# Attention steps on one rotating pool of five PSUM banks, values last in the first two batches, loads staged behind the weights

## The chip, the core and the metric

The kernel runs on one core of a Trainium2 chip. The metric is device time in microseconds (us) of one launch. A profiled execution gives a page and a trace besides. In them PE is TensorE's matmuls, PEld its weight loads, DVE VectorE, ACT ScalarE, POOL GpSimd and SP SyncE, which here only issues DMAs.

## What is computed

Windowed attention for 8 batches of 8 heads, 576 positions, 64 numbers a head, and behind it a two-layer network with a swish on all 4608 tokens (2048 inner columns):

```python
scores = scale * np.matmul(q, k.transpose(0, 1, 3, 2))
rel = pos[:, None] - pos[None, :]
mask_plain = (rel >= 0) & (rel < window)                                    # heads 0 to 3, window 32
mask_dil = (rel >= 0) & (rel < window * dilation) & (rel % dilation == 0)   # heads 4 to 7, dilation 4
scores = np.where(masks[None, :, :, :], scores, -1000000000.0)
attn = softmax(scores)            # written out in the reference
x = (attn @ v), heads side by side, one row a token
h = x @ w_in
out = (h * (1.0 / (1.0 + np.exp(-beta * h)))) @ w_out
```

q, k, v, w_in, w_out and the result are float32; the kernel multiplies in bfloat16.

## The kernel before

**Attention** of one batch is a list of 42 steps, `STEPS` (L16), each named by a letter, a pair of heads (0 and 1 plain, 2 and 3 dilated) and a block. `K` and `Q` (`step_k` L220, `step_q` L229) transpose keys or queries by eight small matmuls into a PSUM bank and copy them out, K on DVE, Q on ACT or DVE by the pair's parity. `S` (L235) multiplies two blocks of scores, takes the exponential on ACT (L255) into `pt`, and multiplies by a mask of zeros and ones on POOL (L256). `V` (L261) multiplies `pt` with values that carry a column of ones, so that the row sums come along, and divides on DVE (L274, L278). `X` (L282) transposes the result, and ACT copies it into `xT`, the input of the network. An `X` needs the `V` steps of its rows; a `V` needs the masks of its scores and the values.

**The network** works in 9 tiles of 512 tokens. A tile has 16 slots `slot_h` (L307: four matmuls, tanh on ACT, L315, and one DVE instruction, L318, that makes `g`) and 16 slots `slot_o` (L333: four matmuls each, four slots to one output block, then a copy on ACT, L346, and a store by SP). `at_once` (L419) says how many of a tile's four output blocks are done within the tile itself; the rest is carried to the next tile. So tile 0 has 16 + 12 slots, tile 1 has 16 + 4 + 8, tile 2 has 16 + 8 + 4, tiles 3 to 6 have 32.

**Order.** Batch 0's attention runs by itself. Then tile t runs slot by slot, and the steps of batch t + 1 are put between the slots in proportion (`room`, `WORK`, L420 to L446), done two slots before the tile's end. Each engine executes its instructions in program order, and the order is that of the program text (`manual_schedule`). Waits are set where an instruction needs data or a buffer that another engine still uses.

**PSUM** has eight banks: `psum_h` 2, `psum_o` 1, `psum_sc` 2 for scores, `psum_pv` 1 for values, `psum_tp` 2 for K, Q and X (L68 to L72).

**Loads.** The plain half of q and k is loaded as float32 by SP into `k_st`, `q_st` and cast by DVE (batch 0) or POOL (L165). The dilated half is loaded and cast in one by POOL's DMAs into `kb`, `qb` (L162). Values are loaded by SP into `vp_st` and `vd_st` (L177, L181, L182) and cast by POOL (`cast_v`, L184); a plain block needs 32 rows of the block before it, which `fill_v` copies from SBUF to SBUF (L192). The weights are loaded and cast by POOL's DMAs, w_in in four pieces (L142) and w_out in four (L147); a piece serves four slots `slot_h`, or one of the four parts of an output block. `extras` (L359) and `first` (L402) hang the loads and casts of later batches on steps: the dilated k of the next batch at `S00`, for instance, and its values two batches ahead.

## Time and profile before

| | |
|---|---|
| time, median of 3 runs | 402.52 us (402.02 to 403.48) |
| the profiled execution's own time | 402.45 us |
| its span | 400.5 us |
| PE busy | 329.2 us, 82% |
| weight loads busy | 173.7 us, 43% |
| DVE busy | 209.0 us, 52% |
| ACT busy | 203.9 us, 51% |
| POOL busy | 168.8 us, 42% |
| read from HBM, written | 39.33 MB, 9.44 MB |

Shares are of the whole span. The span is what the profiler saw from the first instruction to the last; the time of a run has a little around it. A row of a group of instructions reads: line, engine, operation, output<-input, shape, count, then busy time and mean ns of one, then the engine's idle time before them and what ended it. A row of the timeline has its start and length first, and in brackets the idle time before it with the engine that ended it. Matmul ends are modelled, so a busy PE isn't PE at its peak. An average over the span hides that the kernel has stages with different limits.

### The profile page before, as it was taken

The numbers are of one execution on the slowest core, as the hardware profiler recorded it, in microseconds if no ns is written. First come the engines' busy times: TensorE is split into PE (matmuls) and PEld (weight loads), VectorE is DVE, ScalarE is ACT, GpSimd is POOL, SyncE is SP. The second block draws the span as 40 slices with busy tenths as digits, with TensorE's granted clock in tenths as the row PEclk, the third lists the DMA queues.
The fourth block names the chain that finished last, engine by engine and source line by source line (L and its number), as shares of the span: only waits on it lengthen the run. The fifth ranks groups of instructions, "written<-read, shape, count | busy, mean of one in ns | idle before, by whom it ended". The sixth has DMA issues, their size and how long they took to land.

```text
span 400.5 us, 6792 instructions
## 1 busy us (share of the span) xinstructions
PE 329.2 (82%) x2561; PEld 173.7 (43%) x2561; DVE 209.0 (52%) x432; ACT 203.9 (51%) x390; POOL 168.8 (42%) x225
## 2 busy tenths in 40 slices
PE   0525586598898998799989998999899989999995
PEld 0413343254554554355445444544454444444442
DVE  6723377153775586466646664675467544424400
ACT  1413166154765577367636664666466645535521
POOL 8089631885278168407840874077024300000000
PEclk9999999699999999999999999999999999999999
DMA  7979998816731637327333744350000111010022
GB/s 161 208 168 199 210 209 211 201 45 152 182 57 44 164 40 198 103 79 153 112 92 88 139 125 101 82 86 28 28 26 28 26 47 34 26 54 26 26 62 71
DMA packets 47872, 40.96 MB, mean 102 GB/s; under 512 B 22480, under 2 KB 38368, under 8 KB 47840
## 3 DMA queue, kind: packets, MB, share of 16 engines
q1 hardware_dynamic: 37216, 31.62, 30.6%
q0 software_dynamic: 10624, 8.92, 14.8%
q8 instruction: 20, 0.33, 0.4%
q14 instruction: 12, 0.10, 0.1%
HBM read 39.33 MB, written 9.44 MB: 122 GB/s over the span
## 4 chain that ended last, share of the span: by engine, by line
PE 56%; DVE 12%; DMA 10%; ACT 9%; SPq 7%; issue 4%; POOL 1%; ACTq 0%; POOLq 0%
PE o_ps L341 24%; PE h_ps L310 21%; DMA vp_st<-in_v_dram 8%; SPq L177 6%; DVE g L318 5%; ACT tnh L315 4%; PE pv L271 3%; DVE xs L278 3%; PE sc L253 2%; DVE qz L217 2%; PE tp L208 2%; PE h_ps L341 2%; PE tp L287 2%; ACT qz L214 1%; ACT pt L255 1%
## 5 line engine op out<-in xcount | busy, mean ns | idle before, releaser
L318 DVE SCALAR_TENSOR_TENSOR g<-tnh,h_ps 128x512 bf16<-128x512 bf16 x144 | 98.5, 686 | 116.9 <-ACT tnh L315 116.0
L310 PE MATMUL h_ps<-xT,w_in_bf 128*128 128x512 bf16 x576 | 149.1, 385 | 4.6 <-DVE g L318 4.2
L341 PE MATMUL o_ps<-w_out_bf,g 128*128 128x512 bf16 x544 | 137.0, 379 | 2.7 <-ACT osb L346 2.7
L315 ACT ACTIVATE tnh<-h_ps,beta_half 128x512 bf16<-128x512 f32 x144 | 98.5, 688 | 75.7 <-PE h_ps L310 75.1
L310 PEld LDWEIGHTS <-w_in_bf 128*128 128x128 bf16 x576 | 52.4, 99 | 51.5 <-issue 8.7
L341 PEld LDWEIGHTS <-g 128*128 128x128 bf16 x576 | 51.8, 98 | 51.0 <-issue 3.7
L255 ACT ACTIVATE pt<-sc 128x288 bf16<-128x288 f32 (+1 forms) x112 | 49.5, 444 | 33.9 <-PE sc L253 30.9
L256 POOL TENSOR_TENSOR pt<-pt,mask_d 128x288 bf16<-128x288 bf16 x64 | 46.5, 729 | 35.9 <-ACT pt L255 34.9
L271 PEld LDWEIGHTS <-pt 128*128 128x128 bf16 x448 | 23.9, 100 | 63.6 <-DVE xs L278 29.0
L278 DVE TENSOR_TENSOR xs<-pv,rcp 72x256 bf16<-72x256 f32 (+1 forms) x96 | 44.6, 465 | 3.3
L274 DVE RECIPROCAL rcp<-pv 72x4 f32<-72x4 f32 (+1 forms) x96 | 17.2, 179 | 44.7 <-PE pv L271 44.7
L253 PE MATMUL sc<-qz,kT 128*128 128x144 bf16 (+1 forms) x224 | 36.7, 248 | 0.0
L271 PE MATMUL pv<-vd,pt 128*128 128x65 bf16 x256 | 20.0, 200 | 17.7 <-DVE xs L278 14.8
L346 ACT ACTIVATE osb<-o_ps 128x512 f32<-128x512 f32 x34 | 20.4, 600 | 26.2 <-PE o_ps L341 26.2
L271 PE MATMUL pv<-vp,pt 128*128 128x65 bf16 x192 | 12.8, 202 | 21.0 <-POOL pt L256 15.2
L256 POOL TENSOR_TENSOR pt<-pt,mask_PP 128x384 bf16<-128x384 bf16 x32 | 28.6, 913 | 3.2 <-ACT pt L255 3.0
L162 POOL DMA_DIRECT2D kb<-in_k_dram x8 | 6.3, 790 | 54.9 <-PE tp L208 54.1
L297 ACT COPY xT<-tp 128x288 bf16<-128x288 bf16 x32 | 12.7, 397 | 32.7 <-PE tp L287 32.7
L253 PEld LDWEIGHTS <-kT 128*128 128x128 bf16 x224 | 20.4, 103 | 17.1 <-issue 0.5
L287 PE MATMUL tp<-ident_b,xs 72*128 72x72 bf16 (+1 forms) x224 | 21.3, 208 | 5.2 <-DVE xs L278 5.2
L208 PE MATMUL tp<-ident_b,kb 72*128 72x72 bf16 x256 | 14.8, 205 | 10.6 <-DVE kb L169 8.9
L188 POOL CAST vd<-vd_st 128x2048 bf16<-128x2048 f32 x8 | 15.2, 1898 | 19.2 <-PE pv L271 10.9
(52 smaller groups left out, 233.4 us busy)
## 6 DMA issues: line engine op xcount, KB each, us to landing
k_st<-in_k_dram SPq DMA_DIRECT2D x8, 576.0 KB
q_st<-in_q_dram SPq DMA_DIRECT2D x8, 576.0 KB
vp_st<-in_v_dram SPq DMA_DIRECT2D x32, 144.0 KB, 10.1
vd_st<-in_v_dram SPq DMA_DIRECT2D x8, 512.0 KB, 7.0
vd_st<-in_v_dram SPq DMA_DIRECT2D x8, 384.0 KB, 4.7
kb<-in_k_dram POOLq DMA_DIRECT2D x8, 288.0 KB, 5.1
qb<-in_q_dram POOLq DMA_DIRECT2D x8, 288.0 KB, 5.7
w_in_bf<-in_moe_w_in_dram POOLq DMA_DIRECT2D x4, 512.0 KB, 12.1
```

The source lines that it names most:

```text
L177: e(h4).dma_start(out=vp_st[WIN:P, :, h4, :], in_=v[b, h4].rearrange("(i p) d -> p i d", p=QT))
L208: nc.tensor.transpose(tv[:, n], in_, ident_b[0:RT, 0:RT])
L253: nc.tensor.matmul(sc[:, a, 0:2 * n], lhsT=lhsT, rhs=rhs, start=True, stop=True)
L255: nc.scalar.activation(out=w, in_=sc[:, :, 0:2 * n], func=ACT.Exp, scale=SCALE)
L256: nc.gpsimd.tensor_tensor(out=w, in0=w, in1=mask, op=ALU.mult)
L271: nc.tensor.matmul(pv[:, a, h2, :], lhsT=pt[x][:, c:c + P], rhs=rhs, start=True, stop=True)
L278: nc.vector.tensor_tensor(out=xs_t[b, x, jx][:, a0:a0 + m], in0=pv[0:n, :, :, 0:D], in1=rcp[0:n, 0:m].unsqueeze(3).to_broadcast([n, m, 2, ...
L287: nc.tensor.transpose(xp[:, a * n:(a + 1) * n], xs[:, a].rearrange("p h d -> p (h d)"), ident_b[0:n, 0:n])
L310: nc.tensor.matmul(hps[:], lhsT=w_in_bf[:, kt, fb * P:(fb + 1) * P], rhs=xT[:, kt, t * NTOK:(t + 1) * NTOK], start=(kt == 0), stop=(kt == ...
L315: nc.scalar.activation(out=tnh[:], in_=hps[:], func=ACT.Tanh, scale=beta_half[:, fb:fb + 1])
L318: nc.vector.scalar_tensor_tensor(out=g[:], in0=tnh[:], scalar=1.0, in1=hps[:], op0=ALU.add, op1=ALU.mult)
L341: nc.tensor.matmul(ops[:], lhsT=g_t[t, fb][:, tb * P:(tb + 1) * P], rhs=w_out_bf[:, fb, :], start=(fb == 0), stop=(fb == NFB - 1))
```

## The change

- One pool `psum_at` of five banks, taken in turn by every attention step (`bank()`), takes the place of `psum_sc`, `psum_pv` and `psum_tp`. In tile 0 two of three `slot_h` take their bank there too.
- Batches 0 and 1 follow a second list, `STEPS_FIRST`: keys, queries and scores first, values last. Later batches keep `STEPS`.
- In batches 0 and 1 the masks are applied on DVE. In batch 0 all Q copies and the casts of q go to ACT, the casts of v stay on POOL; in batch 1 ACT casts v, at `S23` and `S33`.
- `fill_v` goes: plain values are loaded with all 128 rows of a block, overlap included.
- The weights are all issued by POOL in one go, w_in's first piece behind the first cast of v, the rest behind the second. Batch 1's loads come behind two gates: small DMAs on SP that wait for `g` of slot 1 and of slot 5 of tile 0. Batch 1's q and k are cast at slot 10; batch 2's plain q and k are loaded at slot 18.
- Batch 0's and 1's q and k are loaded in two pieces of 64 and 8 rows.
- Tile 0 does all its output slots itself (32 slots; tile 1 has 24), and batch 1's steps begin at slot 14.
- For later batches, `cast_v` moves into the batch's own `K0` and `K1`, the values of the next batch are loaded at `K2`, both dilated loads at `Q3`.

```diff
+STEPS_FIRST = (
+    "K0 Q0 K1 S00 Q1 S01 K2 S02 Q2 S10 S11 K3 S12 Q3 S20 S21 S22 S23 S30 V00 S31 V01 S32 X00 "
+    "V10 S33 X01 V11 V20 X10 V21 X11 V22 X20 V23 V30 X21 V31 V32 X30 V33 X31"
 ).split()
...
+    FROM = 14
+    GATES = (1, 5)
...
     psum_h = psum("psum_h", 2)
     psum_o = psum("psum_o", 1)
-    psum_sc = psum("psum_sc", 2)
-    psum_pv = psum("psum_pv", 1)
-    psum_tp = psum("psum_tp", 2)
+    psum_at = psum("psum_at", 5)
+
+    def bank(dt=FP32):
+        b = psum_at.tile([P, 512], FP32, name="at")
+        return b[:] if dt == FP32 else b[:].bitcast(BF16)
...
-        nc.vector.memset(vp_st[0:WIN], 0.0)
+        nc.vector.memset(vp_st[0:WIN, 0, 0], 0.0)
...
         if h == 0:
-            stage[b, kind] = stage_pool.tile([RT, 4, R * D], FP32, name=f"{kind}_st")
-            nc.sync.dma_start(out=stage[b, kind][:], in_=src)
-        else:
-            qkb[b, h, kind] = qkb_pool.tile([RT, 4, R * D], BF16, name=f"{kind}b1")
-            nc.gpsimd.dma_start(out=qkb[b, h, kind][:], in_=src)
+            dst = stage[b, kind] = stage_pool.tile([RT, 4, R * D], FP32, name=f"{kind}_st")
+            eng = nc.sync
+        else:
+            dst = qkb[b, h, kind] = qkb_pool.tile([RT, 4, R * D], BF16, name=f"{kind}b1")
+            eng = nc.gpsimd
+
+        for lo, hi in ((0, 64), (64, RT)) if b < 2 else ((0, RT),):
+            eng.dma_start(out=dst[lo:hi], in_=src[lo:hi])
...
             for h4 in range(4):
-                e(h4).dma_start(
-                    out=vp_st[WIN:P, :, h4, :], in_=v[b, h4].rearrange("(i p) d -> p i d", p=QT))
+                if b or h4:
+                    src = bass.AP(tensor=v.tensor, offset=v[b, h4].offset - WIN * D,
+                                  ap=[[D, P], [QT * D, NI], [1, D]])
+                    e(h4).dma_start(out=vp_st[:, :, h4, :], in_=src)
+                else:
+                    src = v[b, h4].rearrange("(i p) d -> p i d", p=QT)
+                    e(h4).dma_start(out=vp_st[WIN:P, :, h4, :], in_=src)
+                    e(h4).dma_start(out=vp_st[0:WIN, 1:NI, h4, :], in_=src[QT - WIN:QT, 0:NI - 1])
...
-    def fill_v(b):
-        va = vp[b % 2]
-        nc.sync.dma_start(out=va[0:WIN, 1:NI], in_=va[96:128, 0:NI - 1])
+
+    def gate(t, fb):
+        nc.sync.dma_start(out=gate_t[:], in_=g_t[t, fb][0:1, 0:16])
...
-        copy = nc.vector.tensor_copy if x % 2 else nc.scalar.copy
+        copy = nc.vector.tensor_copy if b and x % 2 else nc.scalar.copy
...
-        sc = psum_sc.tile([P, 2, 256], FP32, name="sc")
+        sc = bank().rearrange("p (a n) -> p a n", a=2)
...
-        nc.gpsimd.tensor_tensor(out=w, in0=w, in1=mask, op=ALU.mult)
+        eng = nc.gpsimd if b > 1 else nc.vector
+        eng.tensor_tensor(out=w, in0=w, in1=mask, op=ALU.mult)
...
-        hps = psum_h.tile([P, NTOK], FP32, name="h_ps")
+        hps = bank() if t == 0 and fb % 3 else psum_h.tile([P, NTOK], FP32, name="h_ps")[:]
...
     def extras(b):
         e = {}
-        at = lambda name, fn: e.setdefault(STEPS.index(name), []).append(fn)
-        if b + 1 < B:
-            if b:
-                at("K0", lambda: cast_v(b + 1, 0, nc.gpsimd))
-                at("K1", lambda: fill_v(b + 1))
-                at("K1", lambda: cast_v(b + 1, 1, nc.gpsimd))
-            else:
-                at("V30", lambda: cast_v(1, 0, nc.gpsimd))
-                at("V31", lambda: cast_v(1, 1, nc.gpsimd))
-                at("X30", lambda: fill_v(1))
-            at("S00", lambda: load_qk(b + 1, 1, "k"))
+        at = lambda name, fn: e.setdefault((STEPS_FIRST if b < 2 else STEPS).index(name), []).append(fn)
+        G = nc.gpsimd
+        if b:
+            at("S23" if b == 1 else "K0", lambda: cast_v(b, 0, nc.scalar if b == 1 else G))
+            at("S33" if b == 1 else "K1", lambda: cast_v(b, 1, nc.scalar if b == 1 else G))
+        if b and b + 1 < B:
+            at("V11" if b == 1 else "K2", lambda: load_v(b + 1, 0, [nc.sync]))
+            at("V11" if b == 1 else "K2", lambda: load_v(b + 1, 1, [nc.sync]))
+            at("Q3", lambda: load_qk(b + 1, 1, "k"))
             at("Q3", lambda: load_qk(b + 1, 1, "q"))
-            for n, (kind, hp) in zip(("V11", "S30", "S31", "S32") if b else
-                                     ("V20", "V21", "V22", "V23"),
+            for n, (kind, hp) in zip(("V21", "V22", "V30", "V31") if b == 1 else
+                                     ("S30", "S31", "S32", "V30"),
                                      (("k", 0), ("q", 0), ("k", 1), ("q", 1))):
-                at(n, lambda kind=kind, hp=hp: cast_qk(b + 1, kind, hp, nc.gpsimd))
-        if b + 2 < B:
+                at(n, lambda kind=kind, hp=hp: cast_qk(b + 1, kind, hp, G))
+        if b and b + 2 < B:
             at("X31", lambda: load_qk(b + 2, 0, "k"))
             at("X31", lambda: load_qk(b + 2, 0, "q"))
-            last = "X01" if b else "X31"
-            at(last, lambda: load_v(b + 2, 0, [nc.sync]))
-            at(last, lambda: load_v(b + 2, 1, [nc.sync]))
...
-    make_identity(nc, ident_f[:])
     zeros()
     build_masks()
+    make_identity(nc, ident_f[:])
+    for hp in range(2):
+        cast_qk(0, "k", hp, nc.vector)
+        cast_qk(0, "q", hp, nc.scalar)
+    cast_v(0, 0, G)
     load_w_in(0)
...
+    cast_v(0, 1, G)
+    for g in range(1, 4):
+        load_w_in(g)
+    for g in range(4):
+        load_w_out(g)
+    for name in STEPS_FIRST:
         attention_step(0, name)
     build_beta()
...
+    def second(n):
+        if n == GATES[0]:
+            gate(0, n)
+            load_qk(1, 0, "k")
+            load_qk(1, 0, "q")
+            load_qk(1, 1, "k")
+            load_qk(1, 1, "q")
+        if n == GATES[1]:
+            gate(0, n)
+            load_v(1, 0, [SQ])
+            load_v(1, 1, [SQ])
+        if n == 10:
+            for kind, hp in (("k", 0), ("q", 0), ("k", 1), ("q", 1)):
+                cast_qk(1, kind, hp, G)
+        if n == 18:
+            load_qk(2, 0, "k")
+            load_qk(2, 0, "q")
+
+
+    at_once = [4, 2] + [1] * (NTT - 3) + [4]
...
-        work = list(enumerate(STEPS)) if b < B else []
+        steps = STEPS_FIRST if b < 2 else STEPS
+        work = list(enumerate(steps)) if b < B else []
         e = extras(b) if b < B else {}
-        room = [(1 if fn is slot_h else 2) for fn, *_ in slots[:-2]]
+        room = [(1 if fn is slot_h else 2) if t or n >= FROM else 0
+                for n, (fn, *_) in enumerate(slots[:-2])]
...
             fn(*args)
+            if t == 0:
+                second(n)
```

More of the change, by code (lines that the diff above doesn't have):

```diff
@@ L93 @@
     warm = const([P, 1], FP32, "warm")
+    gate_t = const([1, 16], BF16, "gate_t")
     def zeros():
@@ L135, in build_beta @@
     def build_beta():
-        tpb = psum_pv.tile([P, 512], FP32, name="pv")
+        tpb = bank()
         nc.tensor.transpose(tpb[:, 0:NFB], beta_row[:, :], ident_f[:, :])
@@ L168, in cast_qk @@
         for h2 in range(2):
-            eng.tensor_copy(
+            (eng.copy if eng is nc.scalar else eng.tensor_copy)(
                 out=qkb[b, 0, kind][:, hp, :, h2, :],
@@ L199, in transposes @@
         src = qkb[b, h, kind]
-        tp = psum_tp.tile([P, 1024], BF16, name="tp")
+        tp = bank(BF16)
         tv = tp[:, 0:S].rearrange("p (T t) -> p T t", T=R)
@@ L263, in step_v @@
         n, m = (QT, 3) if x < 2 else (HT, 2)
-        pv = psum_pv.tile([P, 512], FP32, name="pv")
-        pv = pv[:, 0:m * 2 * (D + 1)].rearrange("p (m h e) -> p m h e", m=m, h=2)
+        pv = bank()[:, 0:m * 2 * (D + 1)].rearrange("p (m h e) -> p m h e", m=m, h=2)
         for a in range(m):
@@ L284, in step_x @@
         n, m = (QT, 3) if x < 2 else (HT, 4)
-        xp = psum_tp.tile([P, 1024], BF16, name="tp")
+        xp = bank(BF16)
         for a in range(m):
```

31 lines of the change are left out of this document (8 added, 23 removed).

## The prediction, made before the changed kernel was run

> **What bounds the kernel now.** I read the page first (its groups and queues), then one table of busy time by token tile, then the order of time around the start, the chain of work inside a steady tile, and PE's own waits there.
>
> The table's columns are the stretch, its length, then busy us and instructions of PE, weight loads, DVE, ACT and POOL, the granted clock, DMA share and GB/s. I cut it where a tile's last pair of output slots ends:
>
> ```profile
> 0.00:47.85 47.85, 17.42 (x177) 11.99 (x177) 22.14 (x63) 12.32 (x28) 32.84 (x53) 1.00 1.01 187
> 47.85:97.11 49.26, 37.28 (x290) 19.74 (x290) 23.96 (x49) 22.64 (x45) 26.87 (x30) 0.93 0.72 164
> 97.11:134.18 37.07, 33.10 (x290) 18.20 (x288) 23.60 (x48) 22.91 (x45) 20.25 (x26) 1.00 0.50 113
> 134.18:170.66 36.48, 32.23 (x289) 17.63 (x288) 23.38 (x48) 22.77 (x45) 20.17 (x26) 1.00 0.51 121
> 210.07:249.47 39.40, 35.80 (x305) 19.15 (x304) 23.47 (x48) 23.52 (x46) 20.25 (x26) 1.00 0.49 112
> 288.86:328.26 39.40, 35.80 (x306) 19.14 (x304) 23.47 (x48) 23.52 (x46) 11.23 (x14) 1.00 0.11 28
> 328.26:400.50 72.24, 65.94 (x305) 29.56 (x302) 22.00 (x32) 29.16 (x44) 0.00 (x0) 1.00 0.15 44
> ```
>
> So there are four regimes: 47.85 us of attention alone (PE busy 17), tile 0 with batch 1's attention in 49.26 us, tiles 1 to 6 at 36.5 to 39.4 us, and two tiles without attention in 72.24 us. A steady tile takes 39.40 us with POOL at 20.25 and at 11.23 alike: POOL and loads don't set it. What PE must do in a tile, from the chain there (start, length, what):
>
> ```profile
> 216.15 0.17 PE sc L253 x2
> 216.31 0.26 PE tp L208 x8
> 216.57 0.86 PE h_ps L310 x4
> ...
> 229.35 0.19 PE pv L271 x6
> ...
> 240.18 0.13 PE tp L287 x4
> 240.31 0.86 PE o_ps L341 x4
> 241.18 0.13 PE sc L253 x2
> 241.30 0.12 PE pv L271 x4
> ```
>
> A slot is 0.86 us. A batch of attention is 8 x 0.26 + 6 x 0.17 + 8 x 0.13 + 4 x 0.19 + 8 x 0.12 + 8 x 0.13 = 6.9 us. Tile 3 has 32 slots: 27.5 + 6.9 = 34.4 us, so it loses 5.0 of its 39.4. PE's waits in it (us, times, longest) are these:
>
> ```profile
> PE pv L271 <- DVE xs L278: 2.4, 3, 0.9
> PE tp L287 <- DVE xs L278: 0.7, 1, 0.7
> PE tp L208 <- ACT qz L214: 0.5, 1, 0.5
> ```
>
> The first is the single `pv` bank, the third the pair of `tp` banks; the second is data (X31 needs V33). The start is another matter. The queues (packets, MB, share of 16 engines), and three rows in order of time:
>
> ```profile
> q1 hardware_dynamic: 37216, 31.62, 30.6%
> q0 software_dynamic: 10624, 8.92, 14.8%
> ```
> ```profile
> 10.56 0.76 DVE L169 CAST qb<-q_st 72x512 bf16<-72x512 f32 x2 [1.68 <-DMA q_st<-in_q_dram]
> ...
> 21.65 1.46 POOL L186 CAST vp<-vp_st 128x1536 bf16<-128x1536 f32 x1 [11.70 <-DMA vp_st<-in_v_dram]
> ...
> 47.85 1.89 PE L310 MATMUL h_ps<-xT,w_in_bf 128*128 128x512 bf16 x4
> ```
>
> And POOL alone in tile 0, then PE there:
>
> ```profile
> 70.66 1.90 POOL L188 CAST vd<-vd_st 128x2048 bf16<-128x2048 f32 x1 [1.30 <-DMA vd_st<-in_v_dram]
> 72.50 0.80 POOL L162 DMA_DIRECT2D kb<-in_k_dram  x1
> 73.32 0.92 POOL L256 TENSOR_TENSOR pt<-pt,mask_FP 128x384 bf16<-128x384 bf16 x1
> ```
> ```profile
> 74.29 0.35 PE L271 MATMUL pv<-vp,pt 128*128 128x65 bf16 x3 [6.69 <-POOL pt L256]
> ```
>
> DMA's share is 1.01 in the first stretch and 0.72 in the second. POOL waits 11.70 us for batch 0's V, and every mask stands behind it. In tile 0 the same happens again: POOL is stuck behind V casts of a later batch and a load until 73.32, and PE idles 6.69 us for a mask. Tile 0 ideally takes 28 x 0.86 + 6.9 = 31.0 us, so it loses 18.3.
>
> **The change, part by part.** Loads, sized from the shapes: a batch's plain k and q are 1.18 MB, V 0.59 plain (0.79 with 128 rows instead of 96) and 0.92 dilated on SP's queue, and kb and qb 0.59 MB on POOL's. The weights are 4.19 MB on POOL's. The queue rows give a rate for each if it had the engines alone: 31.62 MB in 30.6% of 400.5 us is 258 GB/s, 8.92 MB in 14.8% is 150 GB/s. Check: k and q (4.6 us) plus kb and qb (3.9) from about 2 us end at 10.5; the row says 10.56.
>
> *Batch 0.* With w_in no longer issued ahead of V, plain V lands at 10.5 + 3.1 = 14, dilated V at 17.5. POOL casts (1.46, and 1.90 for the dilated half) end at 15.5 and 19.5. `load_w_in(0)` issues between them, the other seven loads behind, 0.8 us each as the kb issue above. `fill_v` and its wait on POOL go; the longer V rows in their place cost 0.8 us of SP's queue, counted here. The pieces of 64 and 8 rows add issues on queues that wait for data anyway; I count them at nothing. Scores no longer wait for any of this: masks move to DVE and V comes last. What ends last is then ACT, which gets the q casts and all Q copies:
>
> ```profile
> L255 ACT ACTIVATE pt<-sc 128x288 bf16<-128x288 f32 (+1 forms) x14 | 6.2, 448 | 14.7 <-PE sc L253 14.7
> ...
> L214 ACT COPY qz<-tp 64x576 bf16<-64x576 bf16 x2 | 1.3, 633 | 9.8 <-PE tp L208 9.8
> ```
> ```profile
> L278 DVE TENSOR_TENSOR xs<-pv,rcp 72x256 bf16<-72x256 f32 (+1 forms) x12 | 5.6, 464 | 0.4
> L274 DVE RECIPROCAL rcp<-pv 72x4 f32<-72x4 f32 (+1 forms) x12 | 2.2, 183 | 18.5 <-PE pv L271 18.5
> ...
> L122 DVE COPY mask_FP<-mask_PP 128x384 bf16<-128x384 bf16 x1 | 0.3, 260 | 0.0
> ```
>
> From q at 10: four casts on ACT, not in the trace (DVE does one in 0.38, an ACT Q copy of similar size takes 0.63; I take 0.6) to 12.4; 8 x 0.633 + 14 x 0.448 = 11.3 to 23.7; a microsecond of handing over, 25. A mask on DVE lies between a one-input copy of the same shape, 0.26, and POOL's 0.92; I take 0.35, near the copy, so 4.9 us a batch (3.6 to 12.9). DVE's V tail of 12 x (0.464 + 0.183) = 7.8 starts near 23 with four masks (1.4) between: 32.2. X31's copy ends it: the FFN starts at **33** instead of 47.85 (30 to 37).
>
> By the Trainium skill's "SBUF — State Buffer", section "Who interferes with whom", a Vector instruction with two SBUF inputs contends with a GpSimd one that reads SBUF: each mask could then stand behind a POOL cast. Here only two casts, 3.4 us, fall in this stretch, so by that rule the start would be at most 36; the trace of before cannot show it, its DVE operations with two inputs all take one from PSUM.
>
> *Tile 0.* 32 slots now (all its output slots), 27.5 us, and 6.9 of attention, which begins at slot 14. The first h slots run slow: the row at 47.85 has four matmuls in 1.89 us where a slot in the run takes 0.86; I add 2.5 us for three such slots. The granted clock is 0.93 over that stretch. The Trainium skill's "TensorE: Matmul & The Clock Gate", section "What's actually happening", puts half the clock after an idle window until some 3.4 us of work; the row at 47.85 agrees in kind, and by that rule the term would be 1.7 instead of 2.5, and 1.7 more if kb kept PE idle that long again.
>
> h slots need w_in(1..3): from 20 at 3.5 us a group these land at 24 to 31, ahead of use. w_out lands by 45 and is wanted at slots 16 to 19, near 48. The SP gate opens at g(0,1), about 38. Only SP waits there: POOL's kb and qb of batch 1 stand in POOL's queue behind w_out, not behind the gate. From 38 some 10.9 us of POOL's queue and 11.1 of SP's are left, so all has landed at 60 to 61: k and q near 47, kb and qb 52 to 56, plain V 57, dilated V 61. K0 comes after slot 14, at 33 + 2.5 + 15 x 0.86 = 48.4; K2, at slot 17, near 52, so I charge 1.5 us for kb and qb. V's casts on ACT are placed at S23 (near 60) and S33 (near 63): in time. A V cast on ACT isn't in the trace; POOL's take 1.46 and 1.90, DVE's q cast 0.38 with 512 elements a partition against 1536 and 2048, so 1.1 to 2 each, and I take 1.7. Between slots 14 and 31 PE has 15.5 + 6.9 = 22 us; ACT has exponentials, Q and X copies, these casts and four output copies, DVE its K and Q copies, 4.9 of masks and 7.8 of V tail, some 19 to 20 us each by estimate, so I charge 3 us of waits. Tile 0 ends at 33 + 2.5 + 27.5 + 6.9 + 1.5 + 3 = **74.4** (before 97.11, with four slots fewer).
>
> *Tiles 1 to 6.* Five banks in turn: a step waits for the one five steps earlier, about 5 x 0.86 = 4.3 us. The `pv` and `tp` waits, 2.4 + 0.5 = 2.9 us, lose their cause. Late next are DVE and ACT, with 23.5 us each in 37. I take 2.6 for tiles 2 to 6, from 0 (they take the place) to 3.8 (with most of the 1.4 us lost that no wait names). In these tiles masks stay on POOL and cast_v moves to K0 and K1, under POOL's slack shown above; if it came late, the next V00 would wait, some 9 us on. The kb load moves from S00 to Q3, which frees masks that weren't late. SP gets V's loads at K2, behind POOL's casts; output stores behind them have two buffers. Tile 1 has 24 slots: 37.07 - 3.4 - 1.1 = 32.5; I give it less because DVE and ACT have 23 us in 27. Tile 2 is 36.48 - 2.6 = 33.9; tiles 3 to 6 are 4 x 36.8 = 147.2. The last two have no attention and keep 72.2.
>
> *Sum.* 74.4 + 32.5 + 33.9 + 147.2 + 72.2 = 360.2 us of span. The profiled execution took 402.45 with a span of 400.5, so 1.95 lies around it: **362.2**. The median of the runs shown is 402.52, the same for this purpose.
>
> **The rivals.**
> *Batch 1 arrives late.* The gate puts its loads at the end of a full queue. For it: batch 1's V took 18.73 us from its last issue while weights ran beside it:
>
> ```profile
> 32.11 18.73 DMA vp_st<-in_v_dram
> ```
>
> Against: by 50 the weights are out. After the dilated cast some 11 us of V steps and slots remain, so each microsecond later than 61 costs one; at half SP's rate all through it is 11 us: 373.
>
> *The banks weren't the hold.* PE's waits name DVE and ACT as releasers, and with the banks gone PE may simply run into psum_h's two banks and DVE's queue. Then tiles 1 to 6 keep their time: 1.1 + 5 x 2.6 = 14.1, so 376. In that sense the pool would not do what it says. Against: DVE is idle 16 of 39 us in a tile.
>
> *Everything fits.* No charge for kb or waits in tile 0 (-4.5), and the full 3.8 in each of tiles 1 to 6 (-2.7 and -1.2 x 5): 349.
>
> *The pool itself holds PE*, the other side. Before, a score never waited for a K copy; now each step waits in order for a bank of another kind. 42 steps in seven batches are 294 waits. It eats the 40 us gained from a mean of 0.14 us more on each; at 0.16 the time is about 409. Against: the pair of `tp` banks, where a step waits for the one two before it among K, Q and X, costs a tile 0.5 us; five steps back is further than that.
>
> **How the numbers follow.** Forecast 0.44, late batch 0.20, banks not the hold 0.17, everything fits 0.15, the pool holds 0.04 (of which 0.01 ends within 0.5%). A measurement of this kernel tells about 0.5% from no change. Faster 0.96, same 0.01, slower 0.03. The forecast's own range is 355 to 369 (FFN start 30 to 37); with the two rivals of 373 and 376 and most of the 349 one it is 348 to 380, which leaves out the tails of both and the pool's case.
>
> **What would show it.** First h matmul near 33, not 47.85; masks on DVE near 0.35; the gate's first load near 38 and dilated V landed by 61; the first h of tile 1 near 74; steady tiles at 36.8 with no `pv <- xs` waits; the tail unchanged at 72.2. I am wrong if the FFN starts after 37, if ACT waits for a V cast in tile 0, or if a steady tile still takes 39.4.

## The result, and the profile after

| | before | after |
|---|---|---|
| time, median | 403.0 us (402.02 to 405.22, 4 runs) | 368.1 us (366.57 to 372.83, 4 runs) |
| ratio after to before | | 0.911, 95% interval 0.906 to 0.917 |
| the profiled execution's own time, and its span | 402.45, 400.5 us | 368.37, 366.6 us |
| network starts | 47.85 | 34.84 |
| tile 0 ends | 97.11 | 81.85 |
| last two tiles | 72.24 | 71.44 |

The kernel is faster, as forecast, by 34.9 us; the forecast of 362.2 was 5.9 us too low and its range (348 to 380) holds the time. Medians here and below are of all executions of a kernel; the ratios leave out three that took over 1.5% longer than the fastest of their kernel: 372.83 us of the changed kernel, 404.88 of `early_three` and 494.57 of `early_whole_act`.

The same table of busy time by tile as before the change, cut at the same places (stretch, length, busy us and instructions of PE, weight loads, DVE, ACT and POOL, granted clock, DMA share, GB/s):

```profile
0.00:34.84 34.84, 15.61 (x178) 12.49 (x178) 21.39 (x69) 16.71 (x36) 19.68 (x35) 1.00 1.03 182
34.84:81.85 47.01, 39.38 (x306) 20.80 (x306) 30.00 (x63) 26.91 (x48) 13.74 (x20) 0.96 0.99 204
81.85:117.37 35.52, 29.79 (x273) 16.87 (x272) 23.28 (x48) 22.06 (x44) 20.61 (x27) 1.00 0.54 124
117.37:151.19 33.82, 31.75 (x290) 18.01 (x288) 22.99 (x48) 22.56 (x45) 20.59 (x27) 1.00 0.53 126
151.19:187.18 35.99, 34.90 (x305) 19.50 (x304) 23.21 (x48) 23.52 (x46) 20.30 (x26) 1.00 0.50 121
259.16:295.16 36.00, 34.91 (x306) 19.51 (x304) 23.20 (x48) 23.52 (x46) 11.27 (x14) 1.00 0.11 31
295.16:366.60 71.44, 65.93 (x304) 29.58 (x302) 22.02 (x32) 29.17 (x44) 0.00 (x0) 0.99 0.15 45
```

| stretch | before | forecast | after | after minus forecast |
|---|---|---|---|---|
| attention alone | 47.85 | 33.0 | 34.84 | +1.8 |
| tile 0 | 49.26 (28 slots) | 41.4 | 47.01 (32 slots) | +5.6 |
| tile 1 | 37.07 (28 slots) | 32.5 | 35.52 (24 slots) | +3.0 |
| tile 2 | 36.48 | 33.9 | 33.82 | -0.1 |
| tiles 3 to 6, each | 39.40 | 36.8 | 35.99 | -0.8 (four times) |
| last two | 72.24 | 72.2 | 71.44 | -0.8 |

The differences add up to +6.3, rounded, between a span of 366.6 and the forecast's 360.2. The steady tiles came out better than forecast, the first two worse, so the total is nearer than its parts: +10.4 against -4.1. PE's waits in steady tile 3 after the change (us, times, longest) no longer name a bank:

```profile
PE at L309 <- DVE xs L300: 0.7, 1, 0.7
PE o_ps L363 <- ACT osb L368: 0.4, 1, 0.4
```

The 2.4 us on the single `pv` bank and the 0.5 on the `tp` pair are gone; PE is busy 34.9 of 36.0 us. In tile 0 its waits are these:

```profile
PE at L230 <- POOL qb L183: 2.7, 1, 2.7
PE at L230 <- POOL kb L183: 1.6, 1, 1.6
PE at L309 <- DVE xs L300: 1.3, 2, 0.8
PE o_ps L363 <- ACT osb L368: 1.1, 2, 0.7
PE at L293 <- ACT vp L208: 0.9, 1, 0.9
```

The two longest are for batch 1's keys and queries. The timeline shows what happened to them (start, length, and in brackets what ended the engine's idle time):

```profile
39.71 0.61 SPq L216 DMA_DIRECT2D gate_t<-g  x1
40.37 1.19 SPq L176 DMA_DIRECT2D k_st<-in_k_dram  x2
...
49.82 1.17 POOL L183 CAST kb<-k_st 72x512 bf16<-72x512 f32 x2 [16.71 <-DMA k_st<-in_k_dram]
52.95 1.17 POOL L183 CAST qb<-q_st 72x512 bf16<-72x512 f32 x2 [1.97 <-DMA q_st<-in_q_dram]
```

And the chain that ended last, in tile 0, runs over that transfer:

```profile
41.66 0.60 SPq L176
42.26 0.04 issue
42.30 10.54 DMA q_st<-in_q_dram
```

The gate opens 4.9 us after the network's start (the forecast put 5 there), but k and q then need until 52.84. They are 1.18 MB; from 41.0, when SP had issued the first piece, that is 100 GB/s on average, of some 205 GB/s that moved in all. It isn't an even half. The rows of the DMA queues (packets, MB, share of 16 engines; "software" is POOL's queue, "hardware" is SP's) are these from 41 to 43, and then from 45 to 47:

```profile
q0 software_dynamic: 455, 0.41, 124.5%
```
```profile
q1 hardware_dynamic: 206, 0.39, 99.8%
q0 software_dynamic: 15, 0.01, 3.8%
```

Up to 43 POOL's queue, on which the weights and batch 1's dilated k and q were issued, moved everything; from 45 on SP's queue had nearly all. Two kernels of the next section issue these loads later, when POOL's queue is all but done: `masks_pool` at 44.13 and `no_pool` at 46.29. From the issue to the first cast of k it is 6.44 and 6.32 us there and 9.45 here, to the first cast of q 10.70 and 10.03 there and 12.58 here. So some 2 to 3 us of the delay are POOL's queue; the other 10 are what the loads take without it, counted from a late issue. PE idles 4.3 us, and when it goes on it has a lower clock for a while:

```profile
50.00:55.00 5.00, 1.25 (x19) 0.88 (x20) 1.49 (x3) 0.53 (x2) 3.03 (x6) 1.00 0.95 174
55.00:60.00 5.00, 5.00 (x42) 2.84 (x40) 2.43 (x5) 2.34 (x5) 1.36 (x3) 0.66 0.89 256
```

The granted clock is 0.66 over 5 us, 1.7 us lost. The Trainium skill's "TensorE: Matmul & The Clock Gate", section "What's actually happening", has the clock go to half after an idle window of some 3.4 us and back after as much work; the trace agrees: PE was busy 0.43 us between 50 and 54, and the clock was 0.50 from 55 to 58 and 1.00 again from 59.

In tile 1 PE waits for these:

```profile
PE h_ps L332 <- DVE g L340: 3.1, 4, 1.0
PE at L293 <- POOL pt L279: 1.7, 3, 0.8
PE at L309 <- DVE xs L300: 0.7, 1, 0.7
```

At the start, q landed late, and one mask on DVE took 1.62 us beside a cast on POOL, where the others of its shape take 0.34 to 0.36:

```profile
13.24 2.18 ACT L183 CAST qb<-q_st 72x512 bf16<-72x512 f32 x4 [10.94 <-DMA q_st<-in_q_dram]
...
19.00 1.89 POOL L210 CAST vd<-vd_st 128x2048 bf16<-128x2048 f32 x1 [1.08 <-DMA vd_st<-in_v_dram]
19.47 1.62 DVE L279 TENSOR_TENSOR pt<-pt,mask_PP 128x384 bf16<-128x384 bf16 x1 [1.43 <-ACT pt L277]
```

The mask ends 0.2 us after the cast does. So three questions were left: are the banks really what the steady tiles gained from; is it the loads behind the gate that hold tile 0; and what held the start and tile 1.

### The profile page after: what moved, and what is told of

Its sections match the earlier page's. It is cut to its first block, busy times and chain, and to the rows that moved or that the text cites. A ratio compares the mean times of both kernels' runs of the same rounds, so it can differ in the third digit from the quotient of the medians.

```text
span 366.6 us, 6746 instructions
## 1 busy us (share of the span) xinstructions
PE 322.1 (88%) x2561; PEld 175.8 (48%) x2561; DVE 212.5 (58%) x452; ACT 211.5 (58%) x400; POOL 146.8 (40%) x199
## 3 DMA queue, kind: packets, MB, share of 16 engines
q0 software_dynamic: 10432, 8.92, 16.4%
## 4 chain that ended last, share of the span: by engine, by line
PE 72%; DVE 9%; ACT 7%; DMA 6%; issue 2%; POOL 2%; SPq 1%; POOLq 0%; ACTq 0%; DVEq 0%
PE o_ps L363 30%; PE h_ps L332 28%; DMA q_st<-in_q_dram 6%; PE at L230 3%; PE at L275 3%; PE at L293 3%; DVE xs L300 3%; PE at L309 2%; DVE pt L279 2%; PE h_ps L363 2%; DVE g L340 2%; ACT tnh L337 2%; ACT osb L368 1%; POOL pt L279 1%; ACT pt L277 1%
## 5 line engine op out<-in xcount | busy, mean ns | idle before, releaser
L277 ACT ACTIVATE pt<-at 128x288 bf16<-128x288 f32 (+1 forms) x112 | 48.4, 445 | 18.1 <-PE at L275 16.5
L300 DVE TENSOR_TENSOR xs<-at,rcp 72x256 bf16<-72x256 f32 (+1 forms) x96 | 44.6, 465 | 3.3
L275 PE MATMUL at<-qz,kT 128*128 128x144 bf16 (+1 forms) x224 | 35.6, 248 | 2.8 <-DVE kT L239 1.3
L309 PE MATMUL at<-ident_b,xs 72*128 72x72 bf16 (+1 forms) x224 | 22.4, 208 | 9.3 <-DVE xs L300 9.3
L319 ACT COPY xT<-at 128x288 bf16<-128x288 bf16 x32 | 12.7, 397 | 24.0 <-PE at L309 24.0
L230 PE MATMUL at<-ident_b,kb 72*128 72x72 bf16 x256 | 14.8, 205 | 9.7 <-DVE kb L183 8.1
L183 POOL CAST kb<-k_st 72x512 bf16<-72x512 f32 x28 | 16.5, 616 | 16.7 <-DMA k_st<-in_k_dram 16.7
L309 PEld LDWEIGHTS <-xs 72*128 72x128 bf16 (+1 forms) x224 | 14.6, 100 | 17.3 <-DVE xs L300 12.2
L296 DVE RECIPROCAL rcp<-at 72x4 f32<-72x4 f32 (+1 forms) x96 | 17.0, 177 | 9.3 <-PE at L293 8.9
L230 PE MATMUL at<-ident_b,qb 72*128 72x72 bf16 x256 | 14.7, 205 | 8.4 <-ACT qb L183 5.7
```

Source lines behind the costliest of these rows:

```text
L230: nc.tensor.transpose(tv[:, n], in_, ident_b[0:RT, 0:RT])
L275: nc.tensor.matmul(sc[:, a, 0:2 * n], lhsT=lhsT, rhs=rhs, start=True, stop=True)
L277: nc.scalar.activation(out=w, in_=sc[:, :, 0:2 * n], func=ACT.Exp, scale=SCALE)
L300: nc.vector.tensor_tensor(out=xs_t[b, x, jx][:, a0:a0 + m], in0=pv[0:n, :, :, 0:D], in1=rcp[0:n, 0:m].unsqueeze(3).to_broadcast([n, m, 2, ...
L309: nc.tensor.transpose(xp[:, a * n:(a + 1) * n], xs[:, a].rearrange("p h d -> p (h d)"), ident_b[0:n, 0:n])
```

## The experiments

All times are medians, with the ratio to the kernel before on the same chip (403.0 to 403.3 us there) and its 95% interval.

| kernel | time, us | ratio | interval |
|---|---|---|---|
| changed kernel | 368.1 | 0.911 | 0.906 to 0.917 |
| pool_only | 386.76 | 0.958 | 0.956 to 0.961 |
| no_pool | 395.03 | 0.980 | 0.977 to 0.983 |
| early_kq | 362.01 | 0.898 | 0.894 to 0.901 |
| three_blocks | 369.42 | 0.917 | 0.912 to 0.922 |
| whole_qk | 370.97 | 0.921 | 0.916 to 0.925 |
| old_order0 | 369.65 | 0.917 | 0.911 to 0.923 |
| masks_pool | 367.12 | 0.910 | 0.908 to 0.912 |
| early_three | 362.97 | 0.899 | 0.897 to 0.902 |
| early_act | 363.65 | 0.902 | 0.898 to 0.906 |
| early_whole | 363.10 | 0.900 | 0.896 to 0.903 |
| early_whole_act | 359.64 | 0.891 | 0.890 to 0.893 |
| early_whole_act_old0 | 360.25 | 0.894 | 0.892 to 0.896 |

### The pool alone, and all but the pool

`pool_only` is the kernel before with five banks in turn, and nothing else:

```diff
-    psum_sc = psum("psum_sc", 2)
-    psum_pv = psum("psum_pv", 1)
-    psum_tp = psum("psum_tp", 2)
+    psum_at = psum("psum_at", 5)
...
```

The rest of its diff replaces each use of the three pools by `bank()`.

> The kernel before with nothing but the pool of five banks in place of the 2 + 1 + 2. My theory (the separate banks held the steady tiles, and order and loads made the rest): start 47.85 and tile 0 about 49 as before, tiles 3 to 6 at 36.0 as in the changed kernel instead of 39.4, tile 2 near 33.8, so 403 - 4 x 3.4 - 2.7, and up to 2 in tile 1: 385 us. Rival (the banks weren't the hold; the moved loads and casts freed the tiles): steady tiles stay at 39.4 and the time at 403.

386.76 us. The pairs of output slots that end its steady tiles:

```profile
166.87 1.89 PE L342 MATMUL o_ps<-w_out_bf,g 128*128 128x512 bf16 x8
...
202.85 1.89 PE L342 MATMUL o_ps<-w_out_bf,g 128*128 128x512 bf16 x8
...
238.84 1.89 PE L342 MATMUL o_ps<-w_out_bf,g 128*128 128x512 bf16 x8
```

They lie 35.98 and 35.99 us apart, the steady period of the changed kernel. The whole steady gain, 3.4 us a tile, is the pool's. The network starts at 48.35 there: without the rest of the change the pool gains nothing at the start.

`no_pool` is the changed kernel with that diff turned round (two banks for scores, one for values, two for the rest); the h slots of tile 0 take all their banks from `psum_h` again.

> The changed kernel with the old 2 + 1 + 2 banks, all h slots from psum_h. My theory: steady tiles back at 39.4 (13.6 us over four), tile 2 +2.7, and the values at the end of batches 0 and 1, now one after the other through a single bank, some 3 us more in each: 368 + 16 + 6 = 390 us. Rival (the order and the loads carry the gain, the pool little): 368 to 374.

395.03 us, where 390 was expected. Its first wait in PE's list over the whole span:

```profile
PE pv L292 <- DVE xs L299: 25.2, 34, 1.5
```

In the same list of the kernel before it is this:

```profile
PE pv L271 <- DVE xs L278: 19.1, 28, 1.2
```

So the wait on the single bank is 6.1 us longer, and nearly all of that lies in the two stretches with the new order: 6.6 us against 4.7 ahead of the network, 4.6 against 0.7 in tile 0. The pool alone takes 16.6 us off 403.3, the rest of the change alone 8.3, both together 34.9: some 10 us exist only in company. The new order needs the pool, since "values last" puts V steps behind each other on one bank; the network starts at 41.20 there instead of 34.84, and PE's wait list up to then has this row, which the changed kernel's hasn't:

```profile
PE pv L292 <- DVE xs L299: 6.6, 11, 1.0
```

### Loads ahead of the gate

`early_kq` takes batch 1's plain k and q out of the gate; SP issues them right behind `beta`, before the gate has anything to wait for:

```diff
+    load_qk(1, 0, "k")
+    load_qk(1, 0, "q")
     for name in STEPS_FIRST:
...
     def second(n):
         if n == GATES[0]:
-            gate(0, n)
-            load_qk(1, 0, "k")
-            load_qk(1, 0, "q")
```

The first gate goes with them, and the dilated loads stay where they are.

> The changed kernel without the first gate: batch 1's plain k and q are issued by SP right behind beta, as soon as batch 0's casts free the buffers, near 15.5 us. My theory (the gate puts them at the end of a full queue, and PE waits 4.3 us for their casts and then runs some 1.5 us at a lower clock): K0 of batch 1 follows slot 14 at once, tile 0 is 4 to 6 us shorter, 363 us. Rival (DMA is the bound of this stretch, so the wait only moves to kb, qb or the values): 367 to 368. Second rival (the loads push w_in back and the h slots wait): above 368.

362.01 us. The table by tile:

```profile
0.00:33.90 33.90, 16.30 (x178) 12.59 (x180) 21.36 (x70) 16.75 (x36) 19.17 (x34) 1.00 1.08 202
33.90:74.90 41.00, 37.84 (x299) 20.29 (x304) 28.59 (x62) 26.49 (x47) 13.77 (x21) 1.00 1.03 221
74.90:110.42 35.52, 29.54 (x269) 16.87 (x272) 23.28 (x48) 22.03 (x44) 21.01 (x27) 1.00 0.55 125
```

Tile 0 takes 41.00 us instead of 47.01, its clock stays at 1.00, and it ends at 74.90, where the forecast had 74.4. The start is no later for the extra traffic (33.90): the gate guarded nothing that this stretch needed. Tile 1 is not touched.

### Four changes that tile 0 swallowed

Four kernels change something else and leave the gate as it is.

`three_blocks`: `at_once = [3, 2]`, so tile 0 gives four output slots to tile 1.

> The changed kernel with three output blocks in tile 0 instead of four, so 28 and 28 slots in tiles 0 and 1 instead of 32 and 24. My theory (tile 1 at 35.5 us is held by DVE and ACT in its run of 16 h slots, not by PE, so output slots are nearly free there): tile 0 loses 3.4, tile 1 grows by 1 to 2: 366 us. Rival (a slot costs 0.86 wherever it stands): 368. Second rival (tile 0 is held by the loads, so fewer slots don't shorten it): 369 to 370.

`whole_qk`: q and k of batches 0 and 1 in one piece.

```diff
-        for lo, hi in ((0, 64), (64, RT)) if b < 2 else ((0, RT),):
+        for lo, hi in ((0, RT),):
```

> The changed kernel with q and k of batches 0 and 1 loaded whole again instead of in 64 and 8 rows. Before, q had landed when the q cast began on DVE at 10.56; in the changed kernel the q cast on ACT begins at 13.24 (12.3 to 12.6 in other kernels with the two pieces), and the network starts at 34.84 where 33 was forecast. Theory: the small second pieces are what delays q, so with whole loads the q cast begins near 10.6 and the network starts 2 us earlier; tile 0 is held by batch 1's loads behind the gate and gives part of that back; 366 to 367. Rival: q is late because more bytes stand on the two queues at that time (V is no longer behind w_in), not because of the pieces: then the q cast stays near 12.5 to 13 and the time at 368.

`old_order0`: batch 0 follows `STEPS`, batch 1 still `STEPS_FIRST`.

> The changed kernel with batch 0 in the old order STEPS instead of STEPS_FIRST (batch 1 keeps the new one, and everything else stays). Plain V is cast at 17.2 and dilated V at 20.9 in the changed kernel, about when the old order first wants them. Theory (values last matters in batch 0 only while V is late, and V is no longer late; ACT with 23 us of casts, copies and exponentials is the bound, and DVE's V tail of about 8 us is spread under it): the network starts 1 to 3 us earlier than 34.84, tile 0 gives part of it back at its gate, 365 to 368. Rival (values last is what the start lives on; in the old order the V steps stand in PE's and DVE's queues ahead of later K copies and masks): start at 36 to 39, 370 to 374.

`masks_pool`: the masks of batches 0 and 1 on POOL.

```diff
-        eng = nc.gpsimd if b > 1 else nc.vector
+        eng = nc.gpsimd
```

> The changed kernel with the masks on POOL in batches 0 and 1 too. A mask is 0.73 or 0.91 us there and 0.29 to 0.36 on DVE. In batch 0 POOL has two casts of V (3.4 us) and seven weight issues (5.6 us) from 15.7 on, and 14 masks of 11.4 us in all; in tile 0 four casts and two loads beside them. Theory (POOL is the place where batches 0 and 1 were held, and the move of the masks carries the start): the first masks stand behind the casts and issues, the network starts 4 to 8 us later than 34.84 and tile 0 is a few us longer: 374 to 380. Rival (DVE's own load and its waits beside POOL's casts give back what POOL loses): 367 to 370.

None of them beats the changed kernel by more than can be told, `whole_qk` is some 3 us slower, and the forecasts for the time of `three_blocks`, `whole_qk`, `old_order0` and `masks_pool` (366, 366 to 367, 365 to 368, 374 to 380) were all missed, though three of the four mechanisms were there; the times of `three_blocks` and `masks_pool` fell where a rival had put them. First cast of batch 1's plain q on POOL, start of the network, end of tile 0 (us from the span's start):

| kernel | network starts | batch 1's q cast | tile 0 ends |
|---|---|---|---|
| changed kernel | 34.84 | 52.95 | 81.85 |
| three_blocks (28 slots in tile 0) | 33.56 | 52.82 | 85.09 |
| whole_qk | 32.87 | 53.48 | 84.49 |
| old_order0 | 33.14 | 51.52 | 81.34 |
| masks_pool | 39.08 | 54.83 | 81.35 |
| early_kq | 33.90 | 36.76 | 74.90 |

In the first five, over a start from 32.87 to 39.08, batch 1's q is cast within 3.3 us and tile 0 ends within 3.8. The start doesn't set tile 0's end; the arrival of batch 1 does, and `early_kq`, which moves it, moves the end. On the number of slots the row of `three_blocks` says less: it is of that kernel's slowest execution (372.91 us, the others 368.52 to 369.56), in which tile 0 had a mean clock of 0.90 and one long wait of 4.3 us more, shown below. One by one:

`whole_qk`: q of batch 0 does come 2.7 us earlier, and the network starts 2.0 us earlier:

```profile
10.52 2.18 ACT L183 CAST qb<-q_st 72x512 bf16<-72x512 f32 x4 [8.21 <-DMA q_st<-in_q_dram]
```

The pieces are what delays it: the cast begins at 12.11 to 13.43 in the eight traces with pieces, at 10.30 to 10.52 in the four without. The DMA issues of the first 16 us (KB each, median us from issue to landing) show who gained, first in `whole_qk`, then in the changed kernel:

```profile
kb<-in_k_dram POOLq DMA_DIRECT2D x1, 288.0 KB, 10.5
qb<-in_q_dram POOLq DMA_DIRECT2D x1, 288.0 KB, 11.5
```
```profile
kb<-in_k_dram POOLq DMA_DIRECT2D x1, 256.0 KB, 6.6
qb<-in_q_dram POOLq DMA_DIRECT2D x1, 256.0 KB, 10.2
```

In pieces the dilated k on POOL's queue lands 4 us sooner, and the plain q on SP's later, which here is the one wanted first. In tile 0 it is 9.45 us in pieces (40.37 to 49.82) and 11.66 whole (37.87 to 49.53) from SP's issue to the cast of batch 1's k; but the whole load was issued 2.5 us earlier, into more of POOL's traffic, and both casts begin within 0.3 us of each other, so this pair doesn't tell which is quicker. By the Trainium skill's "DMA: Bandwidth & Descriptors", section "Why a DMA increments its semaphore by 16 and not by 1", a transfer of 72 rows would run on 12 engines (the largest divisor up to 16), and one of 64 rows on 16. No row here shows which engines were used, and why the pieces delay q was not tried.

`masks_pool`: the start is 4.2 us later, as forecast (4 to 8), since POOL's first mask stands behind casts and seven weight issues until 25.92; and tile 0 takes 42.3 us instead of 47.0 (PE waits for no k cast there, and the clock stays at 1.00), so that nothing of it is left in the time. That masks went to DVE is worth nothing as long as batch 1 comes late.

`old_order0`: from the q cast (12.11) to the network's start it is 21.03 us, in the changed kernel 21.60. Values last buys nothing in batch 0; V is cast by 17.2 and 20.9 in the changed kernel, about when the old order first wants it.

`three_blocks` also showed what a mask on DVE can cost:

```profile
64.39 1.18 POOL L183 CAST kb<-k_st 72x512 bf16<-72x512 f32 x2
64.47 4.08 DVE L279 TENSOR_TENSOR pt<-pt,mask_PP 128x384 bf16<-128x384 bf16 x1
65.50 1.17 POOL L183 CAST qb<-q_st 72x512 bf16<-72x512 f32 x2
66.62 1.16 POOL L183 CAST kb<-k_st 72x512 bf16<-72x512 f32 x2
67.73 1.28 POOL L183 CAST qb<-q_st 72x512 bf16<-72x512 f32 x2
```

One mask of 0.35 us takes 4.08: it runs from the first to nearly the last of four pairs of casts of batch 2's k and q, and PE waits 4.3 us for the q copy behind it on DVE. This is the rule of the Trainium skill's "SBUF — State Buffer", section "Who interferes with whom", that the prediction weighed: the trace of before couldn't show it, this one agrees with it in kind, though the mask stands behind some seven casts of 0.6 us and not one.

### With the loads early: what is left

`early_three` is `early_kq` with `at_once = [3, 2]`.

> Loads of batch 1's plain k and q ahead of the gate, as in early_kq, and tile 0 with three output blocks at once instead of four. With four blocks and the same loads tile 0 ended at 74.9 and tile 1 took 35.51 with 24 slots, of which 3.1 us were waits for DVE's g and 1.7 for masks; in three_blocks a tile 1 with 28 slots took 36.7, and there tile 0 did not get shorter, being held by the loads. Theory: with the loads early tile 0 has no such hold and gives up its 4 slots, 3.4 us, of which tile 1 takes back 1.2 in place of idle time: about 360. Rival: tile 0 is still held, by batch 1's values or by DVE, and nothing is gained: 362 to 363.

362.97 us, the rival. Tile 0 is only 1.1 us shorter with four slots fewer (35.17 to 75.04), and tile 1, with 28, takes 36.89. With the loads early tile 0 is no longer held by them, but PE's idle time in it grows from 3.2 to 5.0 us: it waits for the batch's own steps on DVE and ACT, for none of them long (1.3 us for `xs`, 0.8 and 0.8 for the V casts on ACT are the longest groups). Which of the two engines it is wasn't told apart.

`early_act` is `early_kq` with batch 2's casts of k and q on ACT:

```diff
-                at(n, lambda kind=kind, hp=hp: cast_qk(b + 1, kind, hp, G))
+                at(n, lambda kind=kind, hp=hp: cast_qk(b + 1, kind, hp, nc.scalar if b == 1 else G))
```

> early_kq with batch 2's casts of plain q and k (which run in tile 0) on ACT instead of POOL. In early_kq the masks on DVE in tile 0 have some of 0.7 to 1.4 us beside POOL's casts, where they otherwise take 0.29 to 0.36. Theory: the masks stand behind POOL's casts; with POOL out of the way all masks in tile 0 have 0.29 to 0.36 us, and DVE's busy time in tile 0 falls by 1 to 2 us; DVE is not what holds PE there (0 to 1 us of waits), so the time goes down by at most 1: 361 to 362. Rival 1: the long masks have another cause (operands, buffer place), and stay. Rival 2: ACT, with 26.5 us of 41 and 4 more now, holds exponentials and Q copies: 363 to 364.

The masks, minimum, median and maximum in ns over batches 0 and 1, first in `early_kq`, then in `early_act`:

```profile
L279 DVE TENSOR_TENSOR pt<-pt,mask_d x16: 293/308/708, 23.3 to 66.6; 128x288 bf16<-128x288 bf16 x16
```
```profile
L279 DVE TENSOR_TENSOR pt<-pt,mask_d x16: 293/308/310, 23.7 to 66.3; 128x288 bf16<-128x288 bf16 x16
```

With ACT casting, no mask of tile 0 is long; the one that is left (1.38 us) lies in batch 0, beside POOL's cast of V. That it is POOL's casts which block them is shown. The time, 363.65, is no better than `early_kq`'s: PE was not waiting for those masks.

`early_whole` is `early_kq` with whole loads.

> Batch 1's plain k and q ahead of the gate (as in early_kq) and all q and k loaded whole (as in whole_qk). In whole_qk the q cast began at 10.52 and the network started at 32.87 instead of 13.24 and 34.84, yet the time did not fall, since tile 0 still waited 3.8 and 3.5 us for batch 1's casts. Theory: the two pieces cost the start about 2 us, and this was hidden only by batch 1's late loads; with these early the 2 us come through: network start 32 to 33, tile 0 41 us, 360. Rival: whole loads also slow what comes after them (weights, values), so that tile 0 gets longer by what the start gains: 362 to 363.

The start falls to 31.85 and tile 0 ends at 72.93, both 2 us earlier than in `early_kq`, so the 2 us of `whole_qk` do come through as far as tile 0's end. The time doesn't show it: 363.10. In tile 1 of the profiled execution the clock falls (stretch, length, busy us, clock, DMA share, GB/s as above):

```profile
100.00:105.00 5.00, 3.22 (x34) 1.89 (x34) 2.49 (x9) 1.69 (x5) 5.00 (x10) 0.94 0.33 79
105.00:110.00 5.00, 4.39 (x22) 1.95 (x21) 0.92 (x3) 0.80 (x2) 3.72 (x3) 0.50 0.78 203
```

A clock of 0.50 over 5 us is 2.5 us. Tile 1 takes 38.3 us here against 35.5 in `early_kq`. Three of the four executions had a mean granted clock of 0.989 to 0.990 and took 362.99 to 363.78; the fourth had 0.999 and took 360.73, the 360 of the theory. `early_kq` has the same split: 361.03 to 362.57 at 0.998 to 1.0, 363.85 at 0.990. PE idles there in either case, while POOL is busy without a gap (5.00 of 5) with masks and casts of batch 3; why the clock falls in one execution and not in another of the same program wasn't settled, and where it fell in the executions without a trace isn't known.

`early_whole_act` takes the POOL casts out of that place too, with `nc.scalar if b < 3` in the diff above.

> early_whole, and the casts of plain q and k of batches 2 and 3, which run in tiles 0 and 1, on ACT instead of POOL. In tile 1 with 24 slots POOL is busy without a gap over the last 9 us (masks 0.73 each between pairs of casts of 1.16), and PE waits 1.7 us for masks there; ACT is busy 22 of 35.5 us. Theory: tile 1 loses its waits for masks and is 1 to 2 us shorter, and tile 0 changes by under 0.5: 1 to 2 us under early_whole, 358 to 359 if that gives 360. Rival: ACT's exponentials and tanh stand behind the casts, each of 0.55 us, and tile 1 gets no shorter: as early_whole or up to 2 us above.

359.64 us, with three executions at 358.96 to 359.86 and a clock of 0.998 to 1.0: the fastest kernel of the study, 8.5 us under the changed kernel. Its trace is of the fourth, so one more run looked at tile 1, with batch 0's old order on top.

> early_whole_act with batch 0 in the old order STEPS. Theory on tile 1 (from early_whole_act, whose undisturbed runs took 358.96 to 359.86 at a mean granted clock of 0.998 to 1.0): with the casts of batch 3 on ACT, PE no longer waits for masks at the end of tile 1, the clock stays at 1.00 there, and tile 1 takes 33.5 to 34.5 us instead of 35.5 to 36.6. On the order: from the q cast to the network's start were 21.0 us in old_order0 and 21.5 in early_whole; V's casts end when the old order first wants them, so the start is 31.4 to 32.4 and the time 358.5 to 360. Rival 1: with q 2 us earlier than in old_order0 the old order now waits for V's casts, 1 to 2 us: 360.5 to 362. Rival 2: tile 1 keeps its 35.5 us and the gain of early_whole_act was only the clock: 361.

360.25 us (359.06 to 361.09): the order of batch 0 makes no difference here either (start 31.93 against 31.85). PE's waits in tile 1 there:

```profile
PE h_ps L332 <- DVE g L340: 3.1, 4, 1.0
PE o_ps L363 <- ACT osb L368: 0.8, 1, 0.8
PE at L309 <- DVE xs L300: 0.7, 1, 0.7
PE at L293 <- POOL pt L279: 0.4, 1, 0.4
```

The 1.7 us for POOL's masks are down to 0.4, the clock over 98 to 113 stays at 1.00, but tile 1 still takes 35.09 us (72.68 to 107.77), not 33.5 to 34.5. What the move gained is probably for the most part the clock: the one execution of `early_whole` at 0.999 took 360.73, those of `early_whole_act` at 0.998 to 1.0 took 358.96 to 359.86, a difference of about 1 us, where the medians differ by 3.5. That is rival 2 in its mechanism, though the time is nearer the theory's. It rests on one execution, and the mean clock alone doesn't order the times: of this last kernel's five, the fastest (359.06) had 0.989. In its trace the clock is 0.50 from 30 to 34, around the network's start; in the changed kernel's the column says 1.00 from 34.84 to 40, yet the network's first four matmuls take 1.89 us in both, where a slot later takes 0.86. So at the start the column isn't to be taken at its word, and a low mean from there costs nothing against the other kernels. 3.1 us remain for `g`: with 24 slots, the 16 h slots run with no carried output slots between them on the two banks of `psum_h`. Whether tile 1 would gain from `bank()` for its h slots, as tile 0 has it, was not tried.

## Why the prediction was right, and where it was off

**Direction and size were right, on the grounds given.** The forecast rested on two things that the profile before showed: an attention stage in which masks stood behind a V cast that waited for loads, and a bank that PE waited for in every steady tile.

- *Steady tiles, forecast 36.8, measured 35.99.* The mechanism is shown by `pool_only`. The size was too small: 2.6 us taken from a range of 0 to 3.8, measured 3.4. The prediction feared that DVE and ACT would be late next; PE's waits there are 1.1 us.
- *Start, forecast 33, measured 34.84.* The term that was off is "q at 10": 13.24, and `whole_qk` shows why, since q came at 10.52 without the two pieces. The prediction counted the pieces "at nothing"; they cost 2.0 us of the start. From q on it took 21.6 us against 23 forecast. What the prediction doesn't name in this stretch is the banks: without the pool the start is 41.20. The sentence on the Trainium skill's SBUF rule (a start of at most 36 by it) held: one mask took 1.62 us.
- *Tile 0, forecast 41.4, measured 47.01.* The step that failed is "k and q near 47, kb and qb 52 to 56, so I charge 1.5". It had k and q come through in 9 us beside POOL's queue, and kb and qb later. It was the other way round: POOL's queue ran first and had kb and qb landed by about 49 (issued up to 32.5 and then 16.4 us to landing), while k and q, issued 2.4 us later than the 38 of the forecast, were there for POOL's casts at 49.82 and 52.95. So the waits were for k and q, where none was forecast, and the charge became 4.3 us of PE's idle time and 1.7 of clock. This is the rival "batch 1 arrives late" in part, by k and q, not by the values on which it was argued; its price was 11 us, 6.0 were paid. The other waits, forecast at 3 us, came to 3.3. `early_kq` shows the rest of the sum: 41.00 without that hold, and 74.90 for its end against 74.4, if not term by term: PE idles 3.2 us there where 4.5 were charged, and is busy 37.84 where the sum has 36.9. The slow first slots came as forecast, though smaller: three of them take 4.1 us in the changed kernel, 1.5 over, against 2.5 in the sum and 1.7 by the Trainium skill's rule. The clock of 0.93 that the prediction set beside them is from elsewhere, from 74 on in the kernel before (0.50 from 74 to 78), behind PE's wait of 6.69 us.
- *Tile 1, forecast 32.5, measured 35.52.* The term was the 28-slot tile's time less four slots' PE time. This tile, whose DVE and ACT have 22 to 23 us, didn't shrink with PE's work: waits for `g` (3.1) and for POOL's masks (1.7) took the place. The prediction saw this coming ("I give it less because DVE and ACT have 23 us in 27") and gave too little: in `early_three` a tile 1 with 28 slots took 36.89, so four slots are worth 1.4 us there and not 3.4.
- *The last two tiles* stayed at 72, as forecast.

Of the things that would have shown it wrong none came: the start was before 37, ACT waited for no V cast in tile 0 (PE did once, 0.9 us, for the cast that ACT makes), and no steady tile took 39.4. ACT's V casts were sized at 1.7 each; they took 1.48 and 1.91.

**Parts that carried nothing.** The forecast credited masks on DVE and values last in batch 0 with the earlier start. `old_order0` shows that the order does nothing there, and `masks_pool` that the masks move the start by 4.2 us but not the time. Of the start's 13.0 us the pool carries 6.4 in company of the new order and the masks 4.2. That the rest is V loaded ahead of the weights is argued and not shown: that part wasn't undone by itself, and neither were the new order of batch 1 or the banks that tile 0's h slots take from the pool.

## What to carry to other kernels

Where several kinds of step use PSUM in a fixed order, let them rotate over one pool instead of a few banks each: it was worth 4% here alone, and the rest of the change was worth less than half as much without it (8.3 us against 18.3). A load that is held back so as not to disturb others needs its own time from the issue on (10 us for 1.18 MB here) and that of what still runs ahead of it on another queue (2 to 3 us here), and what can be loaded ahead of the big transfers without harm (the same 1.18 MB, worth 6 us) should be. When a saving at the start leaves the end of the next stage where it was, look for the transfer that sets it before judging the saving: four edits brought nothing here, and of the three that were tried again with the hold gone one, the whole loads, moved that stage's end by 2 us.

## What the runs showed of the hardware

- A DVE instruction with both inputs in SBUF can stand behind a run of POOL casts, not just one: 4.08 us for a mask of 0.35. The same casts on ACT don't do it (no mask above 0.36 in tile 0).
- Splitting a 72-row load into 64 and 8 rows changed which of two queues was served first: dilated k landed 6.6 us after its issue instead of 10.5, and the cast of plain q began at 12.11 to 13.43 instead of 10.30 to 10.52.
- A load issued on SP's queue from 40.37 on moved nothing up to 43, while POOL's queue moved 0.41 MB in 2 us; from 45 to 47 SP's queue had 0.39 MB and POOL's 0.01.
- The column of the granted clock says 1.00 at the network's start of the changed kernel, while four matmuls take 1.89 us there and 0.86 later.
- A stretch of 5 us at half clock in the middle of the kernel made one tile 38.3 us instead of 35.5 in the one trace that has it; three executions of that program at a mean clock of 0.989 to 0.990 took 362.99 to 363.78, the one at 0.999 took 360.73.
